# Shorter host-ordered steps and an earlier kept-K stage in a two-pass decode attention kernel

## The chip, the cores and the metric

The kernel runs on one core of a Trainium2 chip. The metric is the device time of one execution in microseconds. Before the change it was 1121.21 us, the median of three runs (1120.81 to 1122.77). The profile shows one execution, whose own time is 1120.6 us and whose span from first to last instruction is 1118.8 us.

## What is computed

Two layers of a decode step, run twice with the same weights and the same caches. A is grouped-query attention over a K and a V cache (8 batches, 8 KV heads, 4096 positions, 256 wide, bfloat16: 268 MB together). B is a mixer and an MLP on one token per batch.

```python
def _A_ref(x, k_cache, v_cache, wq, wo):
    q = (x @ wq).reshape(B, Sq, Hq, Dh).transpose(0, 2, 1, 3)
    k = jnp.repeat(k_cache, rep, axis=1)
    v = jnp.repeat(v_cache, rep, axis=1)
    scores = jnp.einsum("bhqd,bhkd->bhqk", q, k) * (Dh ** -0.5)
    p = _softmax(scores, axis=-1)
    o = jnp.einsum("bhqk,bhkd->bhqd", p, v)
    return o.transpose(0, 2, 1, 3).reshape(B, Sq, Hq * Dh) @ wo
...
x = A_x
x = x + _A_ref(_layernorm(x), A_k_cache, A_v_cache, A_wq, A_wo)
x = x + _B_ref(_layernorm(x), B_w1, B_w2, B_w3, B_w4)
x = x + _A_ref(_layernorm(x), A_k_cache, A_v_cache, A_wq, A_wo)
x = x + _B_ref(_layernorm(x), B_w1, B_w2, B_w3, B_w4)
```

With one position per batch the mixer shifts everything away, so B's `hs` is zero and only its norms and its MLP (w3, w4) are left. The second pass over a batch's caches needs the first pass's result for that batch, and nothing of other batches.

## The kernel before

**Items, tasks and places.** A task is (pass, batch, head pair gp), with gp 0 to 3. It has four K items and four V items, each 1 MiB of cache as 128 x 4096 bfloat16. Host code writes the whole order out into `items`. For each item a load goes into one of 15 places in SBUF (`places`, `slots`), and the loop over `items` issues the work on it. When an item's work is issued its place goes back to the list `places`, and `emit_loads()` at the end of each item gives free places to the next loads, all in order on the SP queue (L747, or L722 where two adjacent places take a K pair in one 2 MiB transfer). On the chip the transfer then waits in SP's queue until the work that last used its place is done.

**What one item costs.** A K item that was loaded is transposed in place by VectorE (`transpose_k`, L760: three instructions) and multiplied with the spread q (`scores`, L775: 32 matmuls of 256 columns for a pair in adjacent places, 64 of 128 otherwise); ScalarE takes exponentials (L784). A V item is 16 matmuls (`pv`, L828) with P's columns, which ScalarE spreads into `ptw` (L930) after TensorE transposed P (L811).

**What stays between the passes.** In the first pass of a batch 11 of the 32 places of its caches are kept for the second (`kept`: all eight K's of gp 3 and 2, V 1 to 3 of gp 3). One more V goes through five PSUM banks (`away`, L795, and `back`, L802, four transposes into the place of the first kept K), and a quarter of another in the fifth bank (L1058 and L1071). A second-pass item that is kept needs no load. While a batch is kept, only four places are left for all other loads.

**The chain.** When a batch's first pass is done, its attention output must be scaled, multiplied with wo, normed, sent through the MLP, normed again and multiplied with wq (`chain`, L496 to L509) before the second pass's q exists. These are generators: each `yield` ends a step, and the loop calls `step()` at fixed spots to issue one step of each kind ("chain", "last", "rest") among the attention work. Small vectors go through VectorE, GpSimd (the power in L254) and ScalarE (tanh, L403), products through TensorE: 128 matmuls on wq (L316), 56 on w3 (L383), 56 on w4 (L365), 64 on wo (L365).

**Narrow V's.** Because kept K's can't be used before q, V items saved up from other tasks are put in between: `first_kept` puts `due[:AFTER]` of them into `narrow`, with `AFTER = 12`. There are 16 such V's in the first six batches and 8 in the last two. In a narrow V `step` is called twice: in the middle of its 16 matmuls (`between`) and at its end, both with `calm` true, which means that a step that yielded 2 lets the next call pass without a step. Then the second pass's kept tasks follow (`block(k3)`, `block(k2, k3)`), each K item followed by one item of `due`. If q does not exist when the first kept K's turn comes, `step` is called until it does:

```python
                if ps == 1:
                    while (1, b) not in state:
                        step(10 * len(items))
```

That call issues a step of every kind at each turn. Kept K's are scored in pairs, at the first of the two.

Of the kernel before, what the change touches and what calls it, by code (L numbers as in the profile page):

```python
# [17 lines left out]
def kernel(  # L18
# [33 lines left out]
    Hq = HD // Dh  # L52
# [5 lines left out]
    HC = F // 128  # L58
# [151 lines left out]
    def norm(x, nb, twice):  # L210

        def room(name, shape, at):
            n = shape[0] * shape[1]
            if nb < Bn:
                t = chn.tile([128, n * MID], FP32, tag=name)
                ap = t[:, 0 : n * nb]
            else:
                ap = scratch(at, n * nb)  # L220
            return ap.rearrange("p (s f b) -> p s f b", s=shape[0], f=shape[1])

        def bc(ap):
            return ap.unsqueeze(1).to_broadcast([128, 4, nb])

        xx = room("xx", (2, 4), 0)
        nc.vector.tensor_mul(xx[:, 0], x, wv[:].unsqueeze(2).to_broadcast([128, 4, nb]))
        nc.vector.tensor_mul(xx[:, 1], xx[:, 0], x)
        xs = room("xs", (1, 2), 512)[:, 0]
        nc.vector.tensor_reduce(  # L230
            xs, xx.rearrange("p s f b -> p s b f"), mybir.AxisListType.X, ALU.add
        )
        yield
        st = room_ps("st", nb).rearrange("p (s b) -> p s b", b=nb)
        nc.tensor.matmul(st, ones, xs, start=True, stop=True)
        yield
        mv = room("mv", (1, 2), 528)[:, 0]
        nc.vector.tensor_copy(mv, st)
        var = room("var", (1, 1), 608)[:, 0, 0]
        if nb == 1:  # L240
            nc.vector.scalar_tensor_tensor(
                var, mv[:, 0], mv[:, 0], mv[:, 1], ALU.mult, ALU.subtract, reverse1=True
            )
        else:
            nc.vector.tensor_mul(var, mv[:, 0], mv[:, 0])
            nc.vector.tensor_sub(var, mv[:, 1], var)


        ve = room("ve", (1, 2), 544)[:, 0]
        n = 2 if twice else 1  # L250
        rs = room("rs", (1, 2), 560)[:, 0]

        def power(k0, k1):
            nc.gpsimd.tensor_tensor(  # L254
                rs[:, k0:k1].rearrange("p n b -> p (n b)"),
                ve[:, k0:k1].rearrange("p n b -> p (n b)"),
                nhalf[:].to_broadcast([128, (k1 - k0) * nb]),
                ALU.pow,
            )

        if twice and nb == 1:
            nc.vector.scalar_tensor_tensor(
                ve[:, :, 0], var.to_broadcast([128, 2]), 0.0, eps2[:], ALU.max, ALU.add
            )
            power(0, 2)
        else:
            if twice:
                nc.vector.tensor_scalar(
                    ve[:, 1], var, 0.0, EPS * EPS / (1 + EPS), ALU.max, ALU.add
                )  # L270
                power(1, 2)
            nc.vector.tensor_scalar(ve[:, 0], var, 0.0, EPS, ALU.max, ALU.add)
            power(0, 1)
        xc = room("xc", (1, 4), 576)[:, 0]
        nc.vector.tensor_tensor(xc, x, bc(mv[:, 0]), ALU.subtract)  # L275
        yield 2
        if nb > 1:
            yield
        c = (1 + EPS) ** -0.5 if twice else 1.0
        rl = rs[:, n - 1]  # L280
        parts = ((0, 128, 0, 0, 3, 0), (0, 64, 64, 3, 4, 4), (64, 128, 64, 3, 4, 3))
        if nb == 1:
            nc.vector.scalar_tensor_tensor(
                xbs(1)[:, 0:4, 0], xc[:, :, 0], rl, low[:, int(twice)], ALU.mult, ALU.mult
            )
            parts = parts[1:2]
        for p0, p1, x0, f0, f1, to in parts:
            pp = slice(x0, x0 + p1 - p0)
            dst = xbs(nb)[p0:p1, to : to + f1 - f0, :]
            if nb == 1:  # L290
                nc.vector.tensor_scalar(dst, xc[pp, f0:f1], rl[pp], c, ALU.mult, ALU.mult)
            else:
                nc.vector.scalar_tensor_tensor(
                    dst,
                    xc[pp, f0:f1],
                    c,
                    rl[pp].unsqueeze(1).to_broadcast([p1 - p0, f1 - f0, nb]),
                    ALU.mult,
                    ALU.mult,
                )  # L300
        if twice and nb == 1:
            nc.vector.scalar_tensor_tensor(x, xc, rs[:, 0], x, ALU.mult, ALU.add)
        elif twice:
            nc.vector.tensor_tensor(xc, xc, bc(rs[:, 0]), ALU.mult)
            nc.vector.tensor_add(x, x, xc)
        yield

    def project_q(b0, nb, qT):

        yield from norm(xT[:, :, b0 : b0 + nb], nb, False)  # L310
        q_ps = room_ps("q", nb).rearrange("p (c b) -> p c b", b=nb)
        for j in range(2):
            for h in range(Hq):
                for fc in range(4):
                    w, xi = wblk(wq_sb, HD, 2 * h + j, fc)
                    nc.tensor.matmul(  # L316
                        q_ps[:, j * Hq + h, :],
                        w,
                        xbs(nb)[:, xi, :],
                        start=(fc == 0),  # L320
                        stop=(fc == 3),
                    )
                if h % 8 == 7:
                    yield
        nc.vector.tensor_copy(qT, q_ps)  # L325
        yield

# [27 lines left out]
    def add_cols(y_ps, rhs, w, rows, every, open=None):  # L355

        for fc in range(4):
            at = min(128 * fc, D - 128)
            for i in rows:
                if open is None:  # L360
                    start, stop = i == rows[0], i == rows[-1]
                else:
                    start = open[0] and fc == 0 and i == rows[0]
                    stop = open[1] and i == rows[-1]
                nc.tensor.matmul(  # L365
                    y_ps[:, fc, :],
                    w[:, i, at : at + 128],
                    rhs(i),
                    start=start,
                    stop=stop,  # L370
                    skip_group_check=open is not None,
                )
            if fc % every == every - 1 or fc == 3:
                yield

    def mlp_hidden(b0, nb):

# [2 lines left out]
        for c in range(HC):  # L380
            for fc in range(4):
                w, xi = wblk(w3_sb, F, c, fc)
                nc.tensor.matmul(  # L383
                    h_ps[:, c * nb : c * nb + nb],
                    w,
                    xbs(nb)[:, xi, :],
                    start=(fc == 0),
                    stop=(fc == 3),
                )
            if c % 7 == 6:  # L390
                yield
        g_t = chn.tile([128, 2, HC * MID], FP32, tag="g")
        hh, g0 = g_t[:, 0, 0 : HC * nb], g_t[:, 1, 0 : HC * nb]
        if nb == 1:
# [6 lines left out]
        nc.vector.scalar_tensor_tensor(g0, hh, 2 * 0.044715, h_ps, ALU.mult, ALU.mult)  # L401
        nc.vector.scalar_tensor_tensor(g0, g0, 1.0, h_ps, ALU.add, ALU.mult)
        nc.scalar.activation(g0, g0, ACT.Tanh, scale=0.7978845608028654)  # L403
        yield
        nc.vector.scalar_tensor_tensor(
            HT,
            g0.rearrange("p (c b) -> p c b", b=nb),
# [12 lines left out]
    def z_cols(zall, gps):  # L420
# [14 lines left out]
        yield  # L435
        z_ps = misc[:, 384 : 384 + 4 * np_].rearrange("p (n g) -> p n g", n=4)
        nc.tensor.matmul(z_ps, ones, zm[:], start=True, stop=True)  # L437
        yield
        rz = chn.tile([128, 4, np_], FP32, tag=f"rz{np_}")
        nc.vector.reciprocal(rz[:], z_ps)  # L440
        return rz
# [9 lines left out]
    def half(o_ps, zall, g8, OT, ready):  # L451
# [20 lines left out]
        for j in range(2):  # L472
            nc.tensor.matmul(  # L473
                ot_ps[:, j], o_sb[:].rearrange("p (i j) -> p j i", j=2)[:, j], R[:], start=True, stop=True
            )
        yield
        nc.vector.tensor_copy(OT, ot_ps)
        locked.pop()
        yield
# [60 lines left out]
    keep = sorted({gp for gp, _, _ in kept})  # L540
# [9 lines left out]

    tasks, items, due = [], [], []
    number, narrow = {}, set()
    AFTER = 12

    def block(k, v=None):

        fresh = [(number[v], 1, c) for c in range(4)] if v else []
        if k is None:
            due.extend(fresh)
            items.extend(due)  # L560
            due.clear()
            return
        number[k] = len(tasks)
        tasks.append(k)
        for c in range(4):
            items.append((number[k], 0, c))
            items.extend(due[:1])
            del due[:1]
            if c == 0:
                due.extend(fresh)  # L570

    def first_kept(b, units, before):
# [33 lines left out]
    calm = True  # L606
# [275 lines left out]

    alone = []

    def step(idx, calm=False):

        for kind in ("chain", "last", "rest"):
            e = next((e for e in gens if e["kind"] == kind), None)
            if e is None or (kind == "last" and alone and not e.get("locks") and idx < len(items)):
                continue  # L890
# [3 lines left out]
            if not e["of"] or e["n"] < e["of"] * (idx - e["at"] + 1) / max(e["until"] - e["at"], 1):  # L894
                e["n"] += 1
                had = len(locked)
                got = next(e["g"], gens)
                if len(locked) != had:
                    e["locks"] = len(locked) > had
                e["skip"] = 1 if got == 2 else 0  # L900
# [33 lines left out]
    for idx, it in enumerate(items):  # L934
# [17 lines left out]
        if kv == 0:  # L952
            if (ps, b) not in state:
                if ps == 1:
                    while (1, b) not in state:
                        step(10 * len(items))
                else:
                    state[0, b] = {}
            st = state[ps, b]
# [182 lines left out]
```

## Time and profile before

| what | value |
|---|---|
| median of three runs | 1121.21 us |
| the profiled execution | 1120.6 us, span 1118.8 us |
| TensorE matmul busy | 650.1 us, 58% |
| TensorE weight load busy | 409.6 us, 37% |
| VectorE busy | 603.8 us, 54% |
| ScalarE, GpSimd busy | 162.7 us, 16.4 us |
| mean granted TensorE clock | 0.626 |
| read from HBM | 444.67 MB, 397 GB/s over the span |
| SP waiting for L828, in all | 252.8 us, 146 times |
| SP waiting for L760, in all | 158.7 us, 21 times |

Busy is the time in which an engine had an instruction running; a matmul's end is modelled, so its busy time is not its share of peak. The span is shown in 40 slices of 28 us, each with the data rate of the 16 DMA engines. An idle time in square brackets is what an engine waited before an instruction, and for whom. "SPq" rows are instructions by which SP issues transfers, so the start of such a row is the time at which a place's last user let go.

### The profile page before, as it was taken

The numbers are of one execution on the slowest core, as the hardware profiler recorded it, in microseconds if no ns is written. First come the engines' busy times: TensorE is split into PE (matmuls) and PEld (weight loads), VectorE is DVE, ScalarE is ACT, GpSimd is POOL, SyncE is SP. The second block draws the span as 40 slices with busy tenths as digits, with TensorE's granted clock in tenths as the row PEclk, the third lists the DMA queues.
The fourth block names the chain that finished last, engine by engine and source line by source line (L and its number), as shares of the span: only waits on it lengthen the run. The fifth ranks groups of instructions, "written<-read, shape, count | busy, mean of one in ns | idle before, by whom it ended". The sixth has DMA issues, their size and how long they took to land.

```text
span 1118.8 us, 29781 instructions
## 1 busy us (share of the span) xinstructions
PE 650.1 (58%) x13364; PEld 409.6 (37%) x13364; DVE 603.8 (54%) x1242; ACT 162.7 (15%) x610; POOL 16.4 (1%) x27
## 2 busy tenths in 40 slices
PE   3244467644775446844567446764467546766775
PEld 2122234422453224522345223442244324543555
DVE  4348732587227861478415783259722771585272
ACT  0011111211111110211102111121111111111020
POOL 0000000000000000000000000000000000000000
PEclk9999975855556555655556555575555765555565
DMA  9999999999989999999999999899998999799794
GB/s 360 396 424 428 421 416 383 420 427 421 409 359 425 423 423 411 365 427 427 418 409 373 427 425 417 357 419 423 423 420 356 425 422 418 306 429 416 313 406 199
DMA packets 55808, 446.59 MB, mean 399 GB/s; under 512 B 5881, under 2 KB 9857, under 8 KB 11649
## 3 DMA queue, kind: packets, MB, share of 16 engines
q1 hardware_dynamic: 55488, 444.32, 95.9%
q8 instruction: 104, 1.70, 0.6%
q10 hardware_dynamic: 192, 0.38, 0.1%
q14 instruction: 24, 0.19, 0.0%
HBM read 444.67 MB, written 0.01 MB: 397 GB/s over the span
## 4 chain that ended last, share of the span: by engine, by line
DMA 52%; PE 23%; DVE 18%; SPq 3%; issue 2%; ACT 1%; POOL 0%; DVEq 0%; ACTq 0%
DMA places<-in_A_v_cache_dram 27%; DMA places<-in_A_k_cache_dram 23%; DVE places L760 12%; PE sc L775 9%; PE o L828 7%; PE misc L316 3%; PE misc L365 3%; SPq L174 2%; DVE qbd L339 1%; DVE store L795 1%; DVE places L802 1%; SPq L747 1%; PE misc L473 1%; ACT p_n L784 1%; DMA wq_sb<-in_A_wq_dram 1%
## 5 line engine op out<-in xcount | busy, mean ns | idle before, releaser
L760 DVE STREAM_TRANSPOSE places<-places 128x512 uint32<-128x512 uint32 (+1 forms) x576 | 457.6, 854 | 97.0 <-DMA places<-in_A_k_cache_dram 93.8
L775 PE MATMUL sc<-places,qbd 128*8 128x256 bf16 (+1 forms) x4992 | 248.4, 351 | 230.3 <-DVE places L760 208.9
L828 PE MATMUL o<-places,ptw 128*8 128x256 bf16 x3968 | 241.3, 380 | 175.3 <-DMA places<-in_A_v_cache_dram 149.5
L775 PEld LDWEIGHTS <-qbd 128*8 128x8 bf16 x4992 | 129.1, 104 | 306.5 <-DVE places L760 158.5
L828 PEld LDWEIGHTS <-ptw 128*8 128x8 bf16 x3968 | 102.7, 102 | 246.8 <-issue 158.2
L784 ACT ACTIVATE p_n<-sc 128x256 bf16<-128x256 f32 x128 | 95.2, 744 | 344.2 <-PE sc L775 344.2
L930 ACT COPY ptw<-psv 128x32 bf16<-128x32 bf16 x248 | 50.7, 225 | 213.7 <-PE o L828 212.8
L818 ACT CAST psv<-misc 128x128 bf16<-128x128 f32 x64 | 17.0, 266 | 274.1 <-PE misc L811 274.1
L468 DVE MEMSET o<- 128x256 f32 x31 | 8.4, 272 | 68.6 <-ACT o_sb L467 37.1
L365 PEld LDWEIGHTS <-wo_sb 128*128 128x128 bf16 x1280 | 37.5, 102 | 17.2 <-issue 17.1
L316 PEld LDWEIGHTS <-wq_sb 128*128 128x128 bf16 x1152 | 34.3, 105 | 24.5 <-issue 14.1
L316 PE MATMUL misc<-xb,wq_sb 128*128 128x1 bf16 x1024 | 32.1, 165 | 3.6 <-DVE rz L440 2.3
L784 ACT ACTIVATION_READ_ACCUMULATOR p_n<-sc 128x1 f32 x128 | 33.7, 263 | 0.0
L365 PE MATMUL misc<-OT,wo_sb 128*128 128x1 bf16 x1024 | 30.6, 165 | 3.2 <-issue 2.3
L473 PE MATMUL misc<-R,o_sb 128*128 128x8 f32 x124 | 28.0, 336 | 7.1 <-ACT o_sb L467 7.1
L473 PEld LDWEIGHTS misc<-R,o_sb 128*128 128x128 f32 x124 | 25.3, 283 | 18.9 <-ACT o_sb L467 14.0
L325 DVE CAST qT<-misc 128x32 bf16<-128x32 f32 x8 | 1.5, 192 | 53.4 <-PE misc L316 53.4
L254 POOL TENSOR_TENSOR t<-t,nhalf 128x2 f32<-128x2 f32 (+2 forms) x20 | 14.0, 704 | 1090.1 <-DVE t L275 1090.1
L339 DVE CAST qbd<-misc 32x64 bf16<-32x64 f32 x92 | 19.8, 215 | 18.3 <-PE misc L335 17.3
L440 DVE RECIPROCAL rz<-misc 128x8 f32<-128x8 f32 (+1 forms) x33 | 6.5, 197 | 39.7 <-PE misc L437 21.3
L437 PE MATMUL misc<-zm,one 128*128 128x8 f32 (+1 forms) x66 | 17.7, 341 | 17.3 <-DVE zm L429 9.9
L437 PEld LDWEIGHTS misc<-zm,one 128*128 128x128 f32 x66 | 14.8, 277 | 27.0 <-DVE zm L429 12.4
(104 smaller groups left out, 305.4 us busy)
## 6 DMA issues: line engine op xcount, KB each, us to landing
places<-in_A_v_cache_dram SPq DMA_DIRECT2D x215, 1024.0 KB, 10.9
places<-in_A_k_cache_dram SPq DMA_DIRECT2D x66, 2048.0 KB, 22.9
places<-in_A_k_cache_dram SPq DMA_DIRECT2D x60, 1024.0 KB, 12.5
places<-in_A_v_cache_dram SPq DMA_DIRECT2D x8, 768.0 KB, 4.3
wo_sb<-in_A_wo_dram SPq DMA_DIRECT2D x1, 3584.0 KB
wq_sb<-in_A_wq_dram SPq DMA_DIRECT2D x3, 1024.0 KB
w_sb<-in_B_w_dram SPq DMA_DIRECT2D x1, 1568.0 KB
w_sb<-in_B_w_dram SPq DMA_DIRECT2D x3, 448.0 KB, 11.5
```

What stands on the lines that cost most here:

```text
L174: nc.sync.dma_start(t[:, fc * cols : (fc + 1) * cols], src[fc * 128 : fc * 128 + 128, :])
L316: nc.tensor.matmul(q_ps[:, j * Hq + h, :], w, xbs(nb)[:, xi, :], start=(fc == 0), stop=(fc == 3),)
L339: nc.vector.tensor_copy(qbd[32 * a : 32 * a + 32, :, :, a, :], qs.rearrange("p e (f g u h) -> p (e f) u g h", f=2, u=2, h=2)[:, :, u],)
L365: nc.tensor.matmul(y_ps[:, fc, :], w[:, i, at : at + 128], rhs(i), start=start, stop=stop, skip_group_check=open is not None,)
L437: nc.tensor.matmul(z_ps, ones, zm[:], start=True, stop=True)
L473: nc.tensor.matmul(ot_ps[:, j], o_sb[:].rearrange("p (i j) -> p j i", j=2)[:, j], R[:], start=True, stop=True)
L760: nc.vector.transpose(w, w)
L775: nc.tensor.matmul(sc[32 * k : 32 * k + 8, 128 * x : 128 * (x + nx)], qbd[:, ep, gp].rearrange("p a h -> p (a h)"), v, start=(n == 0), sto ...
L784: nc.scalar.activation(p_sb[:, :, :, 2 * u : 2 * u + 2].rearrange("p t i x -> p x t i"), sc[:, 256 * u : 256 * u + 256].rearrange("p (x t ...
L818: nc.scalar.copy(p_to, pt_ps.rearrange("p t k (a h) -> p a (t k) h", a=4))
L828: nc.tensor.matmul(o_ps[32 * q : 32 * q + 8, :], ptz[:, at : at + 8], v[:, y * Dh : (y + 1) * Dh], start=False, stop=(y >= 12), skip_group ...
L930: nc.scalar.copy(ptw[:, ring_of[it], :, 6:8], psv[slot_of[it[0]]][:, it[2]])
```

## The change

Yields in the chain become `yield 0` where the step after them has no TensorE work; while `calm` is true, `step` goes straight on after a 0. The `yield 2` in `norm` moves from its middle to its end. `AFTER` is 10. In `block`, for a second-pass kept task, the items of `due` come two at a time after the second and the fourth K. The loop that forces a late chain steps only the chain, and with `calm`.

```diff
--- before.py
+++ after.py
@@ -233,7 +233,7 @@
         yield
         st = room_ps("st", nb).rearrange("p (s b) -> p s b", b=nb)
         nc.tensor.matmul(st, ones, xs, start=True, stop=True)
-        yield
+        yield 0
         mv = room("mv", (1, 2), 528)[:, 0]
         nc.vector.tensor_copy(mv, st)
         var = room("var", (1, 1), 608)[:, 0, 0]
@@ -273,7 +273,7 @@
             power(0, 1)
         xc = room("xc", (1, 4), 576)[:, 0]
         nc.vector.tensor_tensor(xc, x, bc(mv[:, 0]), ALU.subtract)
-        yield 2
+        yield 0
         if nb > 1:
             yield
         c = (1 + EPS) ** -0.5 if twice else 1.0
@@ -303,7 +303,7 @@
         elif twice:
             nc.vector.tensor_tensor(xc, xc, bc(rs[:, 0]), ALU.mult)
             nc.vector.tensor_add(x, x, xc)
-        yield
+        yield 2
 
     def project_q(b0, nb, qT):
 
@@ -321,7 +321,7 @@
                         stop=(fc == 3),
                     )
                 if h % 8 == 7:
-                    yield
+                    yield 0 if j == 1 and h == Hq - 1 else None
         nc.vector.tensor_copy(qT, q_ps)
         yield
 
@@ -371,7 +371,7 @@
                     skip_group_check=open is not None,
                 )
             if fc % every == every - 1 or fc == 3:
-                yield
+                yield 0 if fc == 3 else None
 
     def mlp_hidden(b0, nb):
 
@@ -388,7 +388,7 @@
                     stop=(fc == 3),
                 )
             if c % 7 == 6:
-                yield
+                yield 0 if c == HC - 1 else None
         g_t = chn.tile([128, 2, HC * MID], FP32, tag="g")
         hh, g0 = g_t[:, 0, 0 : HC * nb], g_t[:, 1, 0 : HC * nb]
         if nb == 1:
@@ -401,7 +401,7 @@
         nc.vector.scalar_tensor_tensor(g0, hh, 2 * 0.044715, h_ps, ALU.mult, ALU.mult)
         nc.vector.scalar_tensor_tensor(g0, g0, 1.0, h_ps, ALU.add, ALU.mult)
         nc.scalar.activation(g0, g0, ACT.Tanh, scale=0.7978845608028654)
-        yield
+        yield 0
         nc.vector.scalar_tensor_tensor(
             HT,
             g0.rearrange("p (c b) -> p c b", b=nb),
@@ -435,7 +435,7 @@
         yield
         z_ps = misc[:, 384 : 384 + 4 * np_].rearrange("p (n g) -> p n g", n=4)
         nc.tensor.matmul(z_ps, ones, zm[:], start=True, stop=True)
-        yield
+        yield 0
         rz = chn.tile([128, 4, np_], FP32, tag=f"rz{np_}")
         nc.vector.reciprocal(rz[:], z_ps)
         return rz
@@ -473,7 +473,7 @@
             nc.tensor.matmul(
                 ot_ps[:, j], o_sb[:].rearrange("p (i j) -> p j i", j=2)[:, j], R[:], start=True, stop=True
             )
-        yield
+        yield 0
         nc.vector.tensor_copy(OT, ot_ps)
         locked.pop()
         yield
@@ -550,7 +550,7 @@
 
     tasks, items, due = [], [], []
     number, narrow = {}, set()
-    AFTER = 12
+    AFTER = 10
 
     def block(k, v=None):
 
@@ -562,11 +562,14 @@
             return
         number[k] = len(tasks)
         tasks.append(k)
+        two = k[0] == 1 and k[2] in keep
         for c in range(4):
             items.append((number[k], 0, c))
-            items.extend(due[:1])
-            del due[:1]
-            if c == 0:
+            if two and c % 2 == 0:
+                continue
+            items.extend(due[: 1 + two])
+            del due[: 1 + two]
+            if c <= two:
                 due.extend(fresh)
 
     def first_kept(b, units, before):
@@ -882,9 +885,9 @@
 
     alone = []
 
-    def step(idx, calm=False):
-
-        for kind in ("chain", "last", "rest"):
+    def step(idx, calm=False, kinds=("chain", "last", "rest")):
+
+        for kind in kinds:
             e = next((e for e in gens if e["kind"] == kind), None)
             if e is None or (kind == "last" and alone and not e.get("locks") and idx < len(items)):
                 continue
@@ -895,6 +898,8 @@
                 e["n"] += 1
                 had = len(locked)
                 got = next(e["g"], gens)
+                while calm and got == 0:
+                    got = next(e["g"], gens)
                 if len(locked) != had:
                     e["locks"] = len(locked) > had
                 e["skip"] = 1 if got == 2 else 0
@@ -953,7 +958,7 @@
             if (ps, b) not in state:
                 if ps == 1:
                     while (1, b) not in state:
-                        step(10 * len(items))
+                        step(10 * len(items), True, ("chain",))
                 else:
                     state[0, b] = {}
             st = state[ps, b]
```

## The prediction

> **What bounds the kernel now.** I read the page first: the row of transferred bytes over 40 slices, then the queues.
>
> ```profile
> span 1118.8 us, 29781 instructions
> ...
> GB/s 360 396 424 428 421 416 383 420 427 421 409 359 425 423 423 411 365 427 427 418 409 373 427 425 417 357 419 423 423 420 356 425 422 418 306 429 416 313 406 199
> ...
> q1 hardware_dynamic: 55488, 444.32, 95.9%
> ...
> HBM read 444.67 MB, written 0.01 MB: 397 GB/s over the span
> ```
>
> One queue carries nearly everything, and its packets fill 95.9% of the 16 DMA engines' span. Good slices move 420 to 428 GB/s. At 425 GB/s the 444.67 MB need 1046 us, so about 73 us are spent with the stream thin or dry. The weak slices are not random: 383, 359, 365, 373, 357, 356, then 306 and 313, one each time a batch's chain hands over to its second pass. I cut the whole span into windows of 1 us and took, for each below 380 GB/s, the missing share of 425. Eight holes stand out: 2.4 us (from 189), 3.7 (322), 2.8 (456), 3.1 (589), 3.2 (722), 3.3 (855), 7.0 (958), 7.0 (1056): 18.6 us in the first six and 14.0 in the last two, 32.6 in all. Start (3.6) and end (13.9) are not touched by the change. Windows of 2 us through the second hole (columns: TensorE, its weight loads, VectorE, ScalarE, GpSimd busy, granted clock, DMA share, GB/s):
>
> ```profile
> 320.00:322.00 2.00, 1.45 (x18) 0.87 (x18) 0.47 (x3) 0.00 (x0) 0.00 (x0) 0.50 1.02 422
> 322.00:324.00 2.00, 2.00 (x28) 1.35 (x24) 0.65 (x3) 1.45 (x6) 0.00 (x0) 0.50 0.42 164
> 324.00:326.00 2.00, 1.18 (x18) 0.51 (x17) 1.74 (x4) 0.29 (x3) 0.00 (x0) 0.50 0.01 4
> 326.00:328.00 2.00, 0.85 (x10) 0.74 (x14) 1.27 (x5) 0.00 (x0) 0.00 (x0) 0.50 0.84 292
> ```
>
> The engines work and nothing is transferred: no place is free. The timeline before the last hole says why.
>
> ```profile
> 1048.77 0.60 PE L828 MATMUL o<-places,ptw 128*8 128x256 bf16 x8 [0.62 <-DMA places<-in_A_v_cache_dram]
> ...
> 1050.14 0.60 PE L828 MATMUL o<-places,ptw 128*8 128x256 bf16 x8
> 1050.25 0.16 DVE L353 TENSOR_TENSOR xT<-xT,misc 128x4 f32<-128x4 f32 x1 [3.94 <-PE misc L365]
> ...
> 1051.06 0.59 PE L235 MATMUL misc<-t,one 128*128 128x2 f32 x2 [0.32 <-DVE t L230]
> ...
> 1053.25 0.21 DVE L291 TENSOR_SCALAR xb<-t 64x1 bf16<-64x1 f32 x1
> ...
> 1053.63 0.99 PE L316 MATMUL misc<-xb,wq_sb 128*128 128x1 bf16 x32 [1.13 <-DVE rz L440]
> ...
> 1058.77 0.27 PE L335 MATMUL misc<-qT,identb 128*32 128x32 bf16 x4 [0.28 <-DVE qT L325]
> ...
> 1060.03 1.88 PE L775 MATMUL sc<-places,qbd 128*8 128x256 bf16 x32 [0.99 <-DVE qbd L339]
> 1061.94 2.51 DVE L802 STREAM_TRANSPOSE places<-store 128x512 uint32<-128x512 uint32 x4 [1.96 <-PE sc L775]
> 1062.03 3.05 SPq L747 DMA_DIRECT2D places<-in_A_k_cache_dram  x2
> ```
>
> The eighth and last V lands by 1048.77 and is done at 1050.74. Then come norm, q product and q spread, none of which frees a place, and the first kept K's place is handed to a transfer only at 1062.03. Three constants follow. A 1 MiB place takes 1.0486/0.425 = 2.46 us of stream. In the hole of 322 the twelfth V lands at about 314.65 (the eleventh started on landing at 312.19); four more places are 9.8 us, to 324.5, yet the stream ends near 322.8: a landing is seen 1.7 us after its bytes. From issue to flow 1.0 to 1.5 us pass (325.61 to about 326.6; 1062.03 to about 1063.55); I take 1.3. With four places in rotation, three stand behind the V that has just landed, so a place may come back 3 x 2.46 - 1.7 - 1.3 = 4.4 us after its V's landing; each later us is a us without transfer.
>
> **The change part by part.** *Joins (`yield 0`) and the moved skip.* No instruction is added; host steps merge. In the built order the chain then ends with the eighth narrow V, where before it needed twelve V's and a forced rest (or, in the last two batches, eight V's and a forced norm and q product). The price is TensorE time inside those eight V's. From the rows: eight V matmuls 0.53 us start to start, a quarter of q or half of the wo product 0.94, half of w3 or w4 0.84, OT's four 0.95, the statistics 0.52. Latencies that the next product now meets: product end to statistics 0.92 (1050.14 to 1051.06), statistics to xb 2.6 in the first norm and 2.4 in the second (1051.06 to 1053.46), w3's end to HT 1.2 (301.17 to 302.3). On the last batch's landings (1031.00, 1033.40, about 1035.9, 1038.37, 1041.48, 1043.80, 1046.29, 1048.77): V1 and OT done 1033.0, wo to 1033.95; V2 with wo done 1035.95; statistics 1036.34, so xb at 1038.94; V3 done 1037.9, w3 1038.94 to 1039.78 (1.0 idle); V4 with w3 done 1041.7, HT 1042.35 (0.7 idle), w4 to 1043.2; V5 with w4 done 1045.1, statistics 1045.5 to 1046.0, xb 1047.9; V6 done 1047.1, q to 1048.8 (0.8 idle); V7 with q done 1050.8, q to 1051.8; V8 with q done 1053.8. V8's place comes back 5.0 us after its landing, 0.6 beyond 4.4; V7's 4.5, 0.1 beyond. So 0.7 us per batch is paid where before it was nothing.
>
> *First six batches, ten V's.* V9 and V10 hold no chain step and are done at 1055.2 and 1056.2 on the same clock; K0 and K1 (1.9 us of scores, 0.2 of P's transposes) by 1058.4. Four places, V9 to K1, are then issued at least as fast as the stream eats them. The next risk is VectorE's L802 (2.5 us), behind which the next z sums and so V11 stand:
>
> ```profile
> 324.36 2.50 DVE L802 STREAM_TRANSPOSE places<-store 128x512 uint32<-128x512 uint32 x4
> ...
> 326.78 0.12 DVE L426 TENSOR_TENSOR zs_t<-z_t 128x2 f32<-128x2 f32 x1
> ...
> 327.15 0.60 PE L437 MATMUL misc<-zm,one 128*128 128x8 f32 x2 [1.97 <-DVE zm L429]
> ```
>
> V11 is then done near 1062.9; its load must flow by about 1064.9, and 1062.9 + 1.3 leaves 0.7. Covered; without that cover it would cost us for us. Hole left: 0.7 instead of 3.1. Gain 18.6 - 6 x 0.7 = 14.4.
>
> *Last two batches, eight V's as before.* The spread needs 1.26 us to the scores (1058.77 to 1060.03): scores 1055.0 to 1056.9, first hand-back 1057.0 instead of 1062.0. The stream, with V8's late place, ends at 1057.5 and flows again at 1058.3: 0.8. K2's scores now follow a z matmul that waits for L802: 1056.95 + 2.5 + 0.35 + 0.5 = 1060.3, scores to 1062.2, flow 1063.5, while K1's place ends at 1060.8: 2.8. With 0.7 before, 4.3 of each 7.0 stay. Gain 14.0 - 8.6 = 5.4.
>
> *Two places at once, K pairs first.* A kept pair is scored whole with its first K, so K1's place is free without waiting for a V. Some pairs of later K's lose adjacent places: eight pairs in all, 512 matmuls of 128 columns in place of 256 of 256. At the half clock 64 of 128 columns took 1.88 us (at 965.08) and 32 of 256 took 1.88 (at 1060.03): no difference. At the full clock 32 of 256 take about 1.2 (16 in 0.61 at 333.16) against 1.7 to 1.9 for 64 (16 in 0.41 to 0.54 around 1073): 0.7 us a pair, 5.6 in all, if nothing covered it. The stream has 6 to 15 places of its own there, so I take the lower bound, 0. SP gets more single-place K loads; V's are such too and flow at 420 to 428, so 0 again.
>
> *Only a late chain forced.* In the changed order nothing is forced any more. Cost 0; the gain (no L437 and L473 among the q products) is already in the sums.
>
> Sum: 14.4 + 5.4 = 19.8 us off the profiled execution's 1120.6 us (span 1118.8 and 1.8 around it; 0.6 under the median 1121.21): 1100.8. I state 1100.
>
> The granted clock was 0.50 while TensorE was busy 1.81, 2.00 and 1.60 of each 2 us from 312 to 318; only after two full windows from 328 did it show 0.88 and 0.98. The Trainium skill (TensorE: Matmul & The Clock Gate, Part 1: The HAM clock gate) says that some 3.4 us of sustained work lift the clock from half to full. By the row I keep 0.50. By the rule the unbroken stretch from V7 on would turn fast halfway and give V8's place back about 1 us sooner, so all 0.7s would vanish, and the time would be about 1095.
>
> **The rivals.** *All holes close* (22%): L802 and the joins hide entirely; 1120.6 - 32.6 = 1088. For it: the clock may rise with the denser work. Against: the serial 2.5 us of L802 in the last two batches. *Only the first six gain, or only half* (14%): the last two meet L802 and the z matmul in full, and V11 adds a small hole of 1 us in each of six: 1120.6 - 14.4 + 6 = 1112, to 1118 if the pairs cost their 5.6 too. *Slower, by late places* (9%): inside V1 to V8 the latencies are not covered by the V's between. All five laid bare (0.9 + 2.6 + 1.2 + 0.9 + 2.4 = 8.0) against the 3.3 us of idling that my sum has is 4.7 us more at V8, in eight batches 38: 1138. It decides for slower once V8 comes back 7.5 us after landing instead of 5.0 (2.5 x 8 = 20). For it: TensorE is in order, and every V half queues behind a waiting product. Against: each long wait has a whole V before it by order. *No effect* (3%): the stream is limited elsewhere; nothing in the slices says so.
>
> **How the numbers follow.** My forecast, 1093 to 1107, gets 52%. The range of eight in ten runs from all holes closed, 1088, to the half gain, 1111. A measurement of this kernel tells 0.2% (2 us) from no change. Faster: 52 + 22 + 14 = 88%; same 3%; slower 9%.
>
> **What would show it.** Right: no slice from 7 to 35 below about 395 GB/s but two near 380; the first kept scores right behind V10, with L802 after; V8's second half starting about 4.5 us after its landing; holes of under 1 us six times and about 4 twice. Wrong: holes of 2 us or more between V4 and V8 with TensorE idle before L383, L365 or L316; a hole at V11; a thin stream later, where fewer K pairs share a load.

## The result, and the profile after

The changed kernel takes 1111.45 us, the median of four runs (1110.21 to 1112.51), against 1121.99 for the kernel before (four runs, 1120.81 to 1123.34): a ratio of 0.9905, 95% interval 0.9888 to 0.9922. It is faster, by 10.5 us; the forecast was 1100 us, a gain of some 20, and the result lies just above the range's end of 1111. The profiled execution took 1111.91 us.

The page of the changed kernel, the lines that answer to those shown of before:

```profile
span 1109.8 us, 30236 instructions
...
GB/s 359 395 426 425 424 414 360 426 422 425 406 395 425 422 422 385 380 427 422 423 385 421 425 423 418 397 418 424 424 406 393 426 423 414 352 422 421 348 410 160
...
q1 hardware_dynamic: 55776, 444.32, 97.5%
```

The same bytes move in 9.0 us less, but the weak slices are still there: 360 for the first batch's handover (383 before), 380 and 385 further on, and 352 and 348 where 306 and 313 stood.

To see where the time came from I use one measure for every kernel of this study: each window of 1 us counts with the share that it lacks of 425 GB/s, (425 - rate)/425, and all windows are added by stretch, in us. The whole sum follows the span (67.2 - 58.1 = 9.1, against 9.0 of span).

```
                          start   first six   last two   last 25 us   sum    span
before                     6.4      29.2        17.5       14.1       67.2   1118.8
after                      6.5      23.1        12.1       16.5       58.1   1109.8
e1  no joining             6.2      36.9        18.4       15.6       77.1   1128.0
e2  thin products          6.3      10.4         8.2       14.5       39.4   1090.3
e3  AFTER 12               6.6      24.5        12.4       14.6       58.1   1109.2
e4  slower chain           6.5      18.9        11.3       14.3       51.0   1102.8
e5  back later             6.6      22.4         6.8       15.4       51.1   1102.6
e6  one place at a time    6.6      24.9        12.1       15.6       59.1   1110.5
e7  e4 and e5              6.5      13.5         8.3       15.8       44.0   1095.0
e8  one more place         6.3      11.8         7.1       15.2       40.4   1111.0
e9  joins alone            6.3      23.4        12.5       14.0       56.2   1107.8
e10 forcing alone          6.3      24.1        20.6       14.1       65.2   1116.5
```

Start is up to 150 us, first six from there to 910, last two from there on. Each row is one profiled execution; all lie within 2.3 us of their kernel's median but e10's, which is 3.1 above it. The last two batches gained 5.4 us, just what was forecast. The first six gained 6.1 instead of 14.4. That is nearly the whole miss; the rest, 2.4, is the end of the run, which no step of the prediction touches and which varies by as much from kernel to kernel without any order that I can name.

So what is still lost in the first six? Windows of 2 us through the second batch's chain in the changed kernel (columns as in the prediction):

```profile
296.00:298.00 2.00, 2.00 (x61) 1.55 (x60) 0.10 (x1) 0.00 (x0) 0.00 (x0) 0.50 1.01 414
...
300.00:302.00 2.00, 1.98 (x46) 1.03 (x42) 0.44 (x3) 0.00 (x0) 0.00 (x0) 0.50 0.92 360
302.00:304.00 2.00, 1.85 (x20) 1.07 (x21) 0.81 (x6) 0.22 (x1) 0.20 (x1) 0.50 0.95 352
304.00:306.00 2.00, 1.30 (x40) 1.09 (x40) 0.44 (x2) 0.22 (x1) 0.36 (x1) 0.50 0.89 348
306.00:308.00 2.00, 2.00 (x57) 1.28 (x50) 0.00 (x0) 0.07 (x1) 0.00 (x0) 0.50 0.78 250
308.00:310.00 2.00, 2.00 (x65) 1.56 (x63) 0.00 (x0) 0.15 (x1) 0.00 (x0) 0.50 1.01 406
310.00:312.00 2.00, 1.72 (x38) 1.18 (x35) 1.05 (x5) 0.38 (x2) 0.00 (x0) 0.50 0.96 336
312.00:314.00 2.00, 1.78 (x35) 1.02 (x35) 0.00 (x0) 0.06 (x1) 0.00 (x0) 0.56 1.02 348
314.00:316.00 2.00, 0.78 (x22) 0.39 (x20) 1.20 (x2) 1.03 (x4) 0.00 (x0) 1.00 0.97 401
```

There is no dry hole any more like the 4 GB/s of before. Instead the stream is thin, with one good window between: the DMA engines show 0.89 to 0.96 of their time as busy, yet only 336 to 360 GB/s arrive, and 250 in the worst window, at 0.78. The timeline of the same stretch shows which V's these are:

```profile
300.01 0.60 PE L831 MATMUL o<-places,ptw 128*8 128x256 bf16 x8
300.55 0.90 PE L365 MATMUL misc<-HT_t,w_sb 128*128 128x1 bf16 x28
301.38 1.12 PE L831 MATMUL o<-places,ptw 128*8 128x256 bf16 x8
...
308.70 0.60 PE L831 MATMUL o<-places,ptw 128*8 128x256 bf16 x8
309.23 1.01 PE L316 MATMUL misc<-xb,wq_sb 128*128 128x1 bf16 x32
310.18 0.60 PE L831 MATMUL o<-places,ptw 128*8 128x256 bf16 x8
```

The first three lines are V5 with half of w4 between its halves, the last three V8 with the last quarter of q. By the trace's record of transfers V8 landed at 306.06; it is done at 310.78, 4.7 us later (5.0 was forecast). V5's place was handed back at 302.5, and the load that took it was issued at 302.54. That load landed at 309.72, 3.66 us after V8 instead of 2.46. Its turn came when the bytes ahead of it ended, by the prediction's constant 1.7 us before V8's landing was seen: 306.06 - 1.7 = 304.36. It was in the queue 1.8 us before that, and still the stream lost 1.2 us.

The last batch's handover in the changed kernel, from the timeline:

```profile
1045.01 0.60 PE L831 MATMUL o<-places,ptw 128*8 128x256 bf16 x8
...
1046.69 1.88 PE L778 MATMUL sc<-places,qbd 128*8 128x128 bf16 x64 [0.99 <-DVE qbd L339]
1047.74 2.51 DVE L805 STREAM_TRANSPOSE places<-store 128x512 uint32<-128x512 uint32 x4 [1.10 <-PE sc L778]
1048.62 0.33 SPq L750 DMA_DIRECT2D places<-in_A_v_cache_dram  x1
...
1050.68 0.60 PE L437 MATMUL misc<-zm,one 128*128 128x8 f32 x2 [2.11 <-DVE zm L429]
1051.21 1.88 PE L778 MATMUL sc<-places,qbd 128*8 128x256 bf16 x32
...
1053.13 0.80 SPq L750 DMA_DIRECT2D places<-in_A_k_cache_dram  x2
```

The scores now follow V8 directly, and the first place comes back at 1048.62. Then VectorE is in L805 for 2.51 us, the z sums stand behind it, TensorE waits 2.11 us for them, and the next places come back at 1053.13, 4.5 us after the first (forecast: 1057.0 and 1062.2, 5.2 apart). This wait was foreseen as the one that takes the old one's place.

### The profile page after: what moved, and what is told of

Read it like the earlier page. It is cut to its first block, busy times and chain, and to the rows that moved or that the text cites. A ratio compares the mean times of both kernels' runs of the same rounds, so it can differ in the third digit from the quotient of the medians.

```text
span 1109.8 us, 30236 instructions
## 1 busy us (share of the span) xinstructions
PE 646.4 (58%) x13620; PEld 417.2 (38%) x13620; DVE 604.1 (54%) x1242; ACT 160.1 (14%) x610; POOL 16.3 (1%) x27
## 4 chain that ended last, share of the span: by engine, by line
DMA 44%; PE 27%; DVE 20%; SPq 3%; issue 3%; ACT 1%; POOL 1%; DVEq 0%; ACTq 0%
DMA places<-in_A_k_cache_dram 29%; DMA places<-in_A_v_cache_dram 15%; DVE places L763 12%; PE sc L778 8%; PE o L831 8%; PE misc L365 4%; PE misc L316 3%; SPq L174 2%; DVE places L805 2%; DVE store L798 2%; PE misc L383 1%; PE misc L473 1%; SPq L750 1%; DVE qbd L339 1%; POOL t L254 1%
## 5 line engine op out<-in xcount | busy, mean ns | idle before, releaser
L778 PEld LDWEIGHTS <-qbd 128*8 128x8 bf16 x5248 | 136.1, 105 | 321.4 <-DVE places L763 133.7
L316 PEld LDWEIGHTS <-wq_sb 128*128 128x128 bf16 x1152 | 34.8, 104 | 31.1 <-issue 20.9
L365 PEld LDWEIGHTS <-wo_sb 128*128 128x128 bf16 x1280 | 36.9, 102 | 14.8 <-issue 14.7
L316 PE MATMUL misc<-xb,wq_sb 128*128 128x1 bf16 x1024 | 33.5, 165 | 7.7 <-DVE xb L283 5.5
L473 PEld LDWEIGHTS misc<-R,o_sb 128*128 128x128 f32 x124 | 24.5, 275 | 22.3 <-ACT o_sb L467 18.2
L805 DVE STREAM_TRANSPOSE places<-store 128x512 uint32<-128x512 uint32 x32 | 20.1, 684 | 21.4 <-PE sc L778 21.4
L365 PE MATMUL misc<-OT,wo_sb 128*128 128x1 bf16 x1024 | 30.8, 165 | 0.2 <-issue 0.2
L437 PE MATMUL misc<-zm,one 128*128 128x8 f32 (+1 forms) x66 | 17.7, 342 | 21.0 <-DVE zm L429 21.0
L437 PEld LDWEIGHTS misc<-zm,one 128*128 128x128 f32 x66 | 14.8, 279 | 33.0 <-issue 25.6
## 6 DMA issues: line engine op xcount, KB each, us to landing
places<-in_A_v_cache_dram SPq DMA_DIRECT2D x215, 1024.0 KB, 11.8
places<-in_A_k_cache_dram SPq DMA_DIRECT2D x64, 1024.0 KB, 13.5
```

The lines of the kernel that those rows point to most:

```text
L316: nc.tensor.matmul(q_ps[:, j * Hq + h, :], w, xbs(nb)[:, xi, :], start=(fc == 0), stop=(fc == 3),)
L365: nc.tensor.matmul(y_ps[:, fc, :], w[:, i, at : at + 128], rhs(i), start=start, stop=stop, skip_group_check=open is not None,)
L473: nc.tensor.matmul(ot_ps[:, j], o_sb[:].rearrange("p (i j) -> p j i", j=2)[:, j], R[:], start=True, stop=True)
L778: nc.tensor.matmul(sc[32 * k : 32 * k + 8, 128 * x : 128 * (x + nx)], qbd[:, ep, gp].rearrange("p a h -> p (a h)"), v, start=(n == 0), sto ...
L805: nc.vector.transpose(slot[:].bitcast(U32)[:, 512 * n : 512 * n + 512], store[n][:].bitcast(U32))
```

## The experiments

All but two start from the changed kernel, and their diffs are against it. Theory A in the expectations is this: the joins carry the gain; what is left is, in the first six batches, the time of the products that stand between the halves of V4 to V8 and keep places back, and in the last two L805.

**e1: the joining loop taken out.**

```diff
-                while calm and got == 0:
-                    got = next(e["g"], gens)
```

> The changed kernel without the joins: a step that yields 0 ends there again; 10 V's, two places at once and the forcing of the chain alone stay. Theory A (the joins are what gains, because the chain ends by V8, and what they cost is TensorE time inside V2 to V8 that hands places back late): the chain is again unfinished when the kept K's come, two V's earlier than before in six batches, so the long holes return in all eight: 1122 to 1135 us. Rival B (the order of the kept K's and the two places at once gain, and the joins only cost): 1100 to 1111 us.

Measured: 1130.98 us (1129.07 to 1132.76), 1.0075 of before, interval 1.0053 to 1.0098. Without joins the rest of the change is a loss: the chain then needs more V's than the ten it has.

**e9: the joins alone,** in the kernel before (the `yield 0`s, the moved skip and the loop; `AFTER` 12, one place at a time, the old forcing).

> The kernel before with the joining loop alone (and the skip to the next chain moved ahead of it): kept K follow twelve V, one place at a time, the old forcing. Theory A (the joins make the whole gain; the new order of issue, ten V and two places at once are worth nothing): 1109 to 1114 us, 0.988 to 0.993 of before. Rival (the joins pay only together with the new order of issue): 1115 us or more, 0.994 or above.

Measured: 1108.57 us (1108.22 to 1109.63), 0.9884 (0.9869 to 0.9898). The joins make the whole gain. The interval touches that of the full change (0.9888 to 0.9922), so the other parts are worth 1 us at most, or cost up to some 6 us.

**e3: `AFTER` back to 12.**

```diff
-    AFTER = 10
+    AFTER = 12
```

> The changed kernel with kept K's behind 12 V's instead of 10 in the six batches that have 16. Theory A: V1 to V8 are issued as before, and what is lost there stays; V9 to V12 only wait for their landing: within 2 us of the changed kernel, 1109 to 1114 us. Rival D (the loss sits where the kept K's and L805 follow at once on a TensorE that is still behind): two more V's let it catch up, 1103 to 1108 us.

Measured: 1110.5 us (1107.28 to 1113.23), 0.9892 (0.9865 to 0.9918): no difference from the change.

**e6: one place at a time.**

```diff
-        two = k[0] == 1 and k[2] in keep
+        two = False
```

> The changed kernel with one item of due behind every kept K as before, instead of two behind every second. Theory A: the pair is scored at its first K either way, and the places come back at most a V's work (about 1 us) later: within 3 us of the changed kernel, 1110 to 1114 us. Rival F (the two places at once carry a good part of the gain): 1115 us or more.

Measured: 1111.47 us (1108.8 to 1117.79), 0.9906 (0.9877 to 0.9934): no difference, though its six runs scatter over 9 us, and an effect of less than some 5 us would not show. Within that the prediction's 0 for this part holds.

**e10: the forcing alone,** in the kernel before.

```diff
...
-                        step(10 * len(items))
+                        step(10 * len(items), True, ("chain",))
```

> The kernel before with the edit of the forcing alone: a chain is forced ahead of its last head only when it is late. In the prediction this was priced at nothing for the changed kernel, where the chain ends early. Without the joins the chain is further behind, so the forcing is at work here. Theory A (what the forcing moves lies in the last two batches' q product, a step or two of it): 1119 to 1123 us, 0.997 to 1.001. Rival (taking other work out of the last batches gives back part of the 10 us by itself): 1116 us or less, 0.995 or below.

Measured: 1115.22 us (1114.94 to 1118.33), 0.9941 (0.9924 to 0.9957). Theory A's number missed, and the rival's held, but not in the rival's place: in the profiled execution the first six gain 5.1 us and the last two lose 3.1. (That execution is 3.1 us longer than the median, so the loss may be smaller in the others.) The timeline of the kernel before at the second batch's handover (its z matmul of 327.15 is in the prediction):

```profile
320.55 0.59 PE L437 MATMUL misc<-zm,one 128*128 128x8 f32 x2 [0.99 <-DVE qbd L339]
321.08 1.02 PE L775 MATMUL sc<-places,qbd 128*8 128x256 bf16 x16
```

The timeline of e10 there:

```profile
320.94 1.03 PE L775 MATMUL sc<-places,qbd 128*8 128x256 bf16 x16 [0.99 <-DVE qbd L339]
...
323.92 0.58 PE L437 MATMUL misc<-zm,one 128*128 128x8 f32 x2
```

and at the last batch's:

```profile
1050.26 3.72 PE L316 MATMUL misc<-xb,wq_sb 128*128 128x1 bf16 x128 [1.64 <-DVE xb L283]
...
1057.43 2.51 DVE L802 STREAM_TRANSPOSE places<-store 128x512 uint32<-128x512 uint32 x4 [1.96 <-PE sc L775]
...
1060.37 0.60 PE L437 MATMUL misc<-zm,one 128*128 128x8 f32 x2 [2.97 <-DVE zm L429]
```

In this chain the z matmul that the old forcing put ahead of the first kept scores (320.55) comes after them, at 323.92, and waits for nothing; in the kernel before a second one then stood 1.97 us behind L802, at 327.15. In the last batch the first kept scores start 7.8 us after the eighth V is done (1047.71 to 1055.52) instead of 9.3 (1050.74 to 1060.03), but the z matmul thrown out of q lands behind L802 and holds TensorE 2.97 us, so that the second pair's scores start at 1060.90, 5.4 us after the first's instead of 2.8.

**e5: `back` two kept K's later,** so that L805 runs after the second pair's scores and not before them.

```diff
-            if (ps, gp, c) == (1, keep[-1], 1):
+            if (ps, gp, c) == (1, keep[-1], 3):
```

> The changed kernel with the four transposes of L805 issued behind the fourth kept K of the pair instead of the second, so that the z sums and the scores of K2 no longer stand behind 2.5 us of VectorE work. Theory A with the prediction's price for L805: the last two batches gain about 2.8 us each, the first six nothing (V11's load has lead there): 1104 to 1107 us. Rival E (what is left in the last two batches is late V's alone, and L805 delays nothing that a transfer waits for): 1110 to 1112 us.

Measured: 1105.26 us (1104.01 to 1108.85), 0.9849 (0.9827 to 0.9872). The timeline of e5 at the last batch:

```profile
1042.93 1.88 PE L778 MATMUL sc<-places,qbd 128*8 128x128 bf16 x64 [0.99 <-DVE qbd L339]
1044.74 0.60 PE L437 MATMUL misc<-zm,one 128*128 128x8 f32 x2
...
1045.66 1.53 PE L778 MATMUL sc<-places,qbd 128*8 128x256 bf16 x32 [0.32 <-ACT p_n L787]
1046.12 2.47 DVE L805 STREAM_TRANSPOSE places<-store 128x512 uint32<-128x512 uint32 x4
```

L437 waits for nothing now, and the second pair's scores start 2.7 us after the first's instead of 4.5. The last two batches' loss falls from 12.1 to 6.8, the first six's hardly (23.1 to 22.4): the price of L805 lay where the prediction put it.

**e2: the products inside the V's made short.** For a single batch, q and w3 use one of four parts of their sums; three quarters of those sums are left out.

```diff
...
-                for fc in range(4):
+                for fc in range(4) if nb > 1 else (0,):
...
```

> The changed kernel, but for a single batch the q and w3 products use one of the four 128-row parts of their inner dimension: three quarters of those sums are left out (96 of 128 and 42 of 56 matmuls per batch); the order of steps, waits and loads stays. Theory A (places come back late because V2 to V8 carry the whole chain's products): q chunks shrink from 0.94 to about 0.24 us and w3 chunks from 0.84 to 0.21, some 4 us less in front of V8, so its place comes back about 1 us after its landing instead of 5; the thin transfer between V4 and the kept K's goes: 1096 to 1103 us. Rival C (the stretch is slow for the waits between products, for code fetch, or behind L805): at most 4 us gained, 1107 to 1111 us.

Measured: 1094.34 us (1092.12 to 1097.91), 0.9752 (0.9726 to 0.9778), a little below what A expected. The first six fall from 23.1 to 10.4. Windows of e2 through the same chain:

```profile
300.00:302.00 2.00, 2.00 (x40) 1.10 (x40) 0.20 (x1) 0.18 (x1) 0.00 (x0) 0.50 1.05 414
302.00:304.00 2.00, 1.55 (x29) 0.88 (x29) 0.58 (x3) 0.26 (x2) 0.00 (x0) 0.50 1.00 410
304.00:306.00 2.00, 1.03 (x16) 0.52 (x16) 0.47 (x3) 0.22 (x1) 0.00 (x0) 0.50 1.03 426
```

410 to 426 GB/s where the changed kernel had 348 to 360. Here V5's place came back at 297.49, the load before the next one landed at 302.00, so the lead was 302.00 - 1.7 - 297.49 = 2.8 us, and the next load landed 2.50 us later: nothing lost.

**e4: a slower chain.** `AFTER` 12, and in the first six batches the steps after the norms' sums and after HT skip one call, so that a V without a product stands between.

```diff
+        slow[:] = [b] if b < Bn - 2 else []
...
-        yield
+        yield 2 if slow else None
```

> The changed kernel with 12 V's and, in the six batches with 16 V's, a skipped call after the sums of each norm and after the gelu as well, so that no product waits for VectorE or GpSimd and the chain ends with V10 instead of V8. Theory A: V2 to V8 hold one product each at most of the time, no place comes back later than about 3 us after its landing: the thin transfer in six batches falls from about 3.4 us each to about 1: 1097 to 1103 us. Rival C or D (code fetch, L805): no more than 3 us gained, 1108 to 1111 us.

Measured: 1103.13 us (1101.8 to 1104.67), 0.9823 (0.98 to 0.9847). This is just above what A expected, and its place holds in part only: the loss of the first six falls by 4.2 us, to 18.9, where A expected some 14 (from 3.4 to 1 in each of six). The two V's that e3 gave for nothing are worth 7 us when the products are spread over them.

**e7: e4 and e5 together.**

> The spread kernel (12 V's, a skipped call after the norms' sums and the gelu in six batches) with L805 behind the fourth kept K as well. Theory A: both gains add, 1096 to 1100 us. Rival E: as without it, 1102 to 1104 us.

Measured: 1097.95 us (1096.86 to 1099.45), 0.978 (0.9762 to 0.9798). The two gains add up in the times (8.3 and 6.2 us alone, 13.5 together), less well by stretch: the first six fall further than in e4 (13.5 against 18.9), the last two less than in e5 (8.3 against 6.8). It computes all that the kernel before does, and it is the fastest such kernel of this study.

**e8: one more place in rotation.** Ten places kept instead of eleven, so five are left for other loads, and 8 batches read 1 MiB more each.

```diff
-    kept += [(GP - 1, 1, n) for n in range(1, 4)]
+    kept += [(GP - 1, 1, n) for n in range(2, 4)]
```

> The changed kernel with ten places kept instead of eleven (V 1 of head pair 3 is loaded again in the second pass): five places are in rotation during the chain, and 8.4 MB more are read, 19.7 us at 425 GB/s. TensorE's work in the chain is the same. Theory A (the transfer is thin because places come back too late for the next issue): the fifth place gives 2.46 us more, so the thin stretches go, some 15 to 18 us: 1112 to 1117 us, with no slice but start and end below about 410 GB/s. Rival G (dense TensorE work itself slows the transfers, whatever is queued): the thin stretches stay: 1128 to 1133 us.

Measured: 1113.62 us (1111.83 to 1115.27), 0.9918 (0.9899 to 0.9937). The added 8.39 MB need 19.7 us at 425 GB/s, and only 2.2 of them show: 17.5 us of loss are gone (the sum of the table falls by 17.7). Windows of e8:

```profile
304.00:306.00 2.00, 2.00 (x66) 1.56 (x64) 0.00 (x0) 0.00 (x0) 0.00 (x0) 0.50 1.04 434
306.00:308.00 2.00, 2.00 (x57) 1.29 (x54) 0.00 (x0) 0.22 (x1) 0.00 (x0) 0.50 1.00 414
308.00:310.00 2.00, 2.00 (x63) 1.66 (x59) 0.35 (x2) 0.18 (x1) 0.00 (x0) 0.50 1.03 426
```

TensorE is as dense as in the changed kernel, and the stream is full. So it is not the dense work that slows the transfers; it is how early the next load stands in the queue.

## Why the prediction was right, and where it was wrong

**What held.** The stream and its free places bound the kernel, and the joins fill them: e1 and e9 show that they make the whole gain. The order of TensorE's work inside V1 to V8 came out as worked out (in the second chain V6, V7 and V8 were done 3.2, 4.2 and 4.7 us after landing, where the sum has 3.3, 4.5 and 5.0). The last two batches gained 5.4 us, as forecast, with L805 and the z matmul as the wait that takes the old one's place; e5 shows its price, 5.3 us in two batches, 2.7 each, where the prediction's sum had 2.8. Two places at once made no difference that e6 could show, and nothing is forced in the changed kernel.

**What failed: the limit, "a place may come back 3 x 2.46 - 1.7 - 1.3 = 4.4 us after its V's landing; each later us is a us without transfer".** It counts a place that comes back earlier as free. It was drawn from holes, where the queue was empty, and used for a queue that is nearly empty. (For an empty queue its two constants are even too high: 1.7 + 1.3 = 3.0 us, where a lone load measured 2.3, see the end.) I took all loads of 1 MiB in the twelve profiles of this study whose own landing and that of the load ahead are both recorded, and sorted them by lead: how long before its turn (the landing ahead less 1.7) a load was issued. The last column is what the prediction's 1.3 gives at the middle of the row:

```
lead, us      loads   landing after the load ahead, mean us   by the prediction
-2 to -1         3               4.70                              5.26
-1 to 0          4               3.72                              4.26
0 to 1          15               3.13                              3.26
1 to 2          31               3.14                              2.46
2 to 3          61               2.88                              2.46
3 to 4         118               2.57                              2.46
4 to 5         127               2.53                              2.46
```

On the mean a load needs some 3 us of lead, not 1.3, to cost nothing: the limit is about 3 x 2.46 - 1.7 - 3 = 2.7 us after landing. Between 1 and 3 us of lead 0.4 to 0.7 us are lost on the mean, and it is a thin stream, not a dry one. These rows are mixed: of their 92 loads 55 landed within 2.8 us of the load ahead, the others up to 4.3 us after it. So V8 is not alone, with "0.7 us per batch": places that come back 3 to 4 us after landing can cost as well (V5, at a lead of 1.8, paid 1.2 in the second chain). In the first six batches of the changed kernel 71 of 253 loads have both landings recorded. The 11 of them with less than 3 us of lead lost 7.4 us together, where the prediction's 1.3 gives 1.9; e2 has two such loads and e8 one, and they lost 0.1 us.

The first six kept 23.1 of 29.2 us instead of 29.2 - 14.4 = 14.8. Both ways of lifting the lead take most of it away: less product time (e2, first six 10.4), one more place (e8, 11.8). More V's do so only when the chain is spread over them (e4 18.9, e3 24.5). None of the prediction's signs of being wrong names this loss: TensorE idles at most 0.85 us before L383, L365 and L316 in the second chain, and no hole of 2 us is left there. Only the sign of being right is missing: six slices from 7 to 35 lie below 395 (360, 385, 380, 385, 393, 352), where two were to.

In the last two batches the late places show little: without L805 (e5) 6.8 us of loss are left, and the prediction's sum without its 2.8 leaves 17.5 - 14.0 + 2 x 1.5 = 6.5. Why late places cost so much less there was not settled, so that the agreement of the 5.4 is in part luck.

**The forcing.** "Cost 0" was right for the changed kernel, as no step of it is forced. That the edit by itself takes 6.5 us off the kernel before (e10) was not seen: I looked for its effect in the last two batches' q product, and there the profiled execution loses.

**The clock.** The rule of the Trainium skill (TensorE: Matmul & The Clock Gate, Part 1: The HAM clock gate), that some 3.4 us of sustained work lift the clock, would have had V8 done earlier. In the changed kernel TensorE was busy 2.00, 2.00 and 1.72 of 2 us from 306 to 312 and the granted clock stayed at 0.50; it read 1.00 only from 314 on, after V8. Keeping 0.50 was right.

**The rivals.** "Only the first six gain, or only half" named the right time, 1112, by the wrong place: V11's hole. "Slower, by late places" had the right place, V4 to V8, but by another cause (bare waits of TensorE) and at too high a price; without the joins (e1) the kernel is slower.

## What to carry to other kernels

Where a stream of loads must stay full with few buffers, measure at which lead a load costs nothing in a row of loads, not only how long an empty queue takes to start: here some 3 us on the mean, more than the time of one load. Count then every buffer that comes back inside that lead, not only the latest. Shorter steps pay once; after that, spread the long ones evenly over the buffers, and look which engine's copy stands ahead of the next hand-back.

## What the runs showed of the hardware

A load of 1 MiB that met an empty queue landed 4.7 to 4.8 us after its issue (4.69 at 1062.0 in the kernel before, 4.71 at 958.5 in the changed one), 2.3 more than its 2.46 of bytes. The Trainium skill (DMA: Bandwidth & Descriptors, Anatomy of one DMA) gives some 2.0 us of fixed cost for each transfer. It does so for transfers that GpSimd issues; these are issued by SyncE, and the 2.3 lie near it. A fixed cost does not tell that a load already queued 1 to 3 us ahead lands 0.4 to 0.7 us late on the mean. Why the stream thins there was not settled.

One rival for this is left untested. Among the data the trace has transfers of 16 KB on the instruction queue:

```profile
q8 instruction: 106, 1.74, 0.6%
```

In the twelve profiles 56 of the 937 loads with 3 us of lead or more landed over 2.8 us after the load ahead; 55 of these 56 had such a transfer start within 2.5 us of the landing ahead, and of all 937 only 483 had. With 1 to 3 us of lead the 72 loads with one landed 3.03 us after the load ahead, mean, the 20 without 2.76. e8 has 105 of these transfers and a full stream, so by themselves they do not thin it. Whether they do where few loads are queued was not tried; e2, which has fewer matmuls, also has fewer of them, 98.

TensorE also stopped once in the middle of the third batch's q product in the changed kernel, for 1.99 us, waiting for nothing that the profile shows:

```profile
441.48 0.77 PE L316 MATMUL misc<-xb,wq_sb 128*128 128x1 bf16 x23
444.24 0.38 PE L316 MATMUL misc<-xb,wq_sb 128*128 128x1 bf16 x9 [1.99 <-issue]
```

The stretch from 416 to 550 us, which holds it, lost 5.1 us in windows below 380 GB/s, its neighbours 2.6 and 2.5. One of the 16 KB transfers started at 441.82, 0.4 us before TensorE stopped at 442.25; whether that held it was not tried.
